# Five places in VectorE's order, in the experts' part of an attention and two-layer mixture-of-experts kernel

## The chip, the cores and the metric

The kernel runs on one core of a Trainium2 chip. The metric is the device time of one execution in microseconds (us), lower is better. TensorE (PE, with its weight loads PEld) multiplies matrices, VectorE (DVE) and ScalarE (ACT) work on elements, GpSimd (POOL) here starts the gathers and scatters by row index, and SyncE (SP) starts the other transfers. Each engine takes its own instructions in the order in which the program lists them and waits for the others by semaphores.

## The reference, cut to what matters

```python
def reference(**kwargs):                       # three layers, one after the other
    attn_out = _attn_ref(**attn_kwargs)        # a gated linear attention, 4 x 8 heads, 768 steps, 48 wide
    x = attn_out.transpose(0, 2, 1, 3).reshape(B * S, H * D)     # 3072 rows of 384
    x = _moe_ref(x=x, **moe_kwargs)            # experts, stage 1
    return _moe2_ref(x=x, **moe2_kwargs)       # experts, stage 2, with a bias on the logits by modality

def _moe_ref(x, w_gate, w1, w2):               # N, D, E, F = 3072, 384, 8, 1024
    logits = x @ w_gate
    expert_idx = np.argmax(logits, axis=1)
    probs = softmax(logits)                    # (a sum of exponentials plus 1e-9)
    gate_w = probs[np.arange(N), expert_idx]
    for e in range(E):
        mask = expert_idx == e
        h = np.maximum(x[mask] @ w1[e], 0.0)
        out[mask] = gate_w[mask, None] * (h @ w2[e])
    return out
```

Each row goes through one expert alone, so the kernel sorts the rows by expert on the chip and works on tiles of 128 rows of one expert.

## The kernel before

**Arithmetic.** The inputs are float32. Each matrix product is made of three float16 products: a number is split into a high half and a low half, and high x high, high x low and low x high are added. So the weights `ws` have a high part `wh` (ScalarE, line 746, 128x768 at a time) and a low part `wl` (VectorE, line 747), and the hidden layer of a tile has `hh` (ScalarE, line 827) and `hl` (VectorE, line 828).

**A tile.** A tile of 128 rows goes through `Stage.steps`: for each quarter q of the 1024 hidden columns, `g1_q` (18 matmuls, into one of three banks `mpq`, `mpk`, `msc`), `hh_q`, `hl_q`, and `g2_q` (six matmuls into `mpu` or `mpy`; the third and the sixth read `hl`). At the end `ev` (VectorE, line 840) makes the factor of each row and `yo` (ScalarE, line 843) scales the output, which POOL scatters. While tile j runs, the kernel also prepares later ones: a gather for tile j+3 (`ga`), the scaling of tile j+2 (`sq` on ScalarE; `sv` on VectorE, lines 775 to 778, four instructions on `ev` and `xs`), the transposes of tile j+1 (`T` on PE; `xh`; `xl`), and the logits of the next layer for the rows that are done (`la` to `ld`).

**Weights.** When the next tile belongs to another expert, the parts of its weights replace the old ones step by step. A part is named by `h` (high) or `l` (low), the matrix (0 for w1, 1 for w2) and the quarter, so `l11` is the low part of the second quarter of w2. Each part stands in an `If` on a register (`Stage.tile`, line 858), since whether the expert changes is known only on the chip. The four last parts (positions of 10 and more in `CHG`) are made in the next tile. SP loads the weights themselves (`refill`).

**Order.** The program order of every engine is written by hand. `POS[stage]` gives each step of a tile a position from about -2 to 10, `CHG[stage]` does so for the weight parts, and `EXT` for everything that stands beside the tiles: an entry's tens count tiles, its rest is the position, and a list holds the positions of the pieces of a generator, one after another. `Stage.tile` sorts all of a tile's pieces by position and emits them, and each engine takes its own in that order.

**Beside the tiles.** `R1` and `R2` are the routers of the two stages. `tabling` makes a table of registers (which expert, whether it changes), in five pieces; `gating` makes the row factors in four: an exponential (ScalarE), eight instructions on VectorE (lines 539 to 547), a strip of 24 or 31 matmuls of 62 columns (PE, line 551), and seven instructions that read it (lines 553 to 562; `ev` and `yo` need what they make).

**Stages and branches.** The first tiles of a stage (two in stage 1, four in stage 2) run "ahead", before the routing is complete, on the expert that is likeliest to come first. `Stage.ahead` then has a branch (line 888) for the case that the guess was wrong; every engine reads a register of the table and passes the branch, and PE's next matmul waits for those engines whose data could have been written in it. `Stage.run` does the remaining tiles. Those from 24 on stand in nested `If`s (line 914), as only the chip knows how many there are; here stage 1 has tiles 0 to 28 and stage 2 tiles 0 to 24. At the end of a stage PE waits again at these `If`s. Stage 1 makes the first weights of stage 2 in its last tile; the parts with positions from 10 on are then made in tile 0 of stage 2, by the entry `wsp`.

Of the kernel before, what the change touches and what calls it, by code (L numbers as in the profile page):

```python
# [25 lines left out]
NT = N // P  # L26
# [78 lines left out]
def attention(tc, ctx, C, q, k, v, a_re, a_im, wg, flags, emit_y, emit_lg, extra, ps, inp):  # L105
# [271 lines left out]


POS=[dict(r1=-1.031,g1_0=0,hh_0=0.547,g1_1=0.882,hl_0=1.39,la=2.05,hh_1=2.196,g1_2=2.293,g2_0=2.443,lc=2.732,hl_1=3.114,r2=4.038,hh_2=4.156,T=4.338,
    g2_1=4.65,xh=4.8,hl_2=4.8,xl=5.173,sq=5.3,g1_3=5.65,hh_3=5.721,lb=5.802,g2_2=6.338,sv=6.511,lt=6.833,ga=6.883,ev=7.217,hl_3=7.445,ld=7.7,  # L380
    g2_3=8.105,yo=9.966),
    dict(la=-2.149,ga=-2.099,r1=-1.063,g1_0=-0.801,g1_1=-0.106,hh_0=1.2,hh_1=2.2,hl_0=2.367,hl_1=2.614,g1_2=2.928,T=3.282,r2=3.634,g2_0=3.64,lc=3.664,
    hh_2=4.688,xh=4.798,hl_2=4.8,xl=5.2,g1_3=5.366,sq=5.443,lb=5.487,g2_1=5.99,hh_3=6.083,hl_3=7.1,ev=7.3,g2_2=7.5,lt=7.586,ld=7.7,sv=7.978,g2_3=8.5,
# [4 lines left out]
    dict(h00=1.25,l00=2.555,h01=3.772,l01=3.889,h10=5,l10=5.85,h02=6.908,h11=7.334,l02=7.573,h03=8.381,l11=8.43,l03=9.238,h12=11.713,h13=12.469,l12=12.6,  # L388
    l13=13.5)]

EXT=dict(ga1=[9.894],tab1=[10.675,11.888,14.575,16.434,19.076],sc2=[14.852,16.409],tu2=[17.791,18.391,19.266],
    sc3=[16.942,20.231],gate1=[13.14,22.34,23.74,26.94],bias=[38.314],guess=[7.193,9.387],ec=[1.828,2.259,3.158],es=[5.811,7.12,9.347],eg0=[-0.314],
    eg1=[2.518],eg2=[2.797],eg3=[0.24],esc0=[7.854,8.86],esc1=[9.262,9.598],esc2=[17.6,18.2],esc3=[17.787,19.2],etu0=[10.7,10.819,11.2],etu1=[16.719,
    16.834,17.692],etu2=[20.882,21.035,21.741],etu3=[26.7,26.797,29.053],wsp=[0.41],lgl=[1.567,2.117,4.049,5.381,7.217],bat=[11.965,12.932,13.065,
    16.165],fin2=[15.779,17.6,18.5,21.1,21.3],ga2=[21.761],tab2=[18.791,23.611,24.661,26.111,28.111],scE=[31.762,31.857],tuE=[34.33,34.944,35.562],
    scF=[34.804,36.2],gate2=[33.763,38.234,40.083,40.999],ckw=[5.75,7.75],ck=[8.464])


HINT=1.5; DRAIN=6.9
# [289 lines left out]
class Rot:  # L689
# [3 lines left out]
    def tile(s, *a, **kw):  # L693
        k=s.i%len(s.t); s.i+=1
        return s.get(k)
# [4 lines left out]
class Bufs:  # L700
# [16 lines left out]
    def rest(s, sb):  # L717
        sh=lambda n,shape,dt,nm: Rot(n,lambda k: sb.tile(shape,dt,name=f"{nm}{k}",tag=f"{nm}{k}",bufs=1))
        s.xg=sh(4,[P,DM],F32,"xg"); s.xs=sh(2,[P,DM],F32,"xs"); s.ev=sh(4,[P,4],F32,"ev")
        s.xh=sh(2,[P,ND,P],F16,"xh"); s.xl=sh(2,[P,ND,P],F16,"xl")  # L720
        s.yo=sh(3,[P,DM],F32,"yo"); s.lxT=sh(6,[P,ND,P],F32,"lxT")
# [27 lines left out]
class Stage:  # L749
# [98 lines left out]
    def tile(s, j, mid=(), old=None, chg=None, refill=False, **kw):  # L848


        W=s.W
        st=[(s.pos[k],f) for k,f in s.steps(j,**kw).items()]

        for k,p in s.chg.items():
            c=old if p>=10 else chg
            if c is None: continue
            def part(c=c,k=k):
                with s.tc.If(c["hl".index(k[0])]!=0): W.split(((int(k[1]),int(k[2])),),**{"lo" if k[0]=="h" else "hi":False})  # L858
            st.append((p%10,part))
        if refill:  # L860
            rf=s.refill(j-1)
            for k in ("r1","r2"): st.append((s.pos[k],lambda: next(rf)))
        st.extend(mid)
        st.sort(key=lambda t:t[0])
        for _,f in st: f()
# [194 lines left out]
def attention__moe__moe2_kernel(tc, q, k, v, a_re, a_im, w_gate, w1, w2, mid, w_gate2, mbias, out):  # L1060
    nc=tc.nc
    with ExitStack() as ctx:
# [8 lines left out]
        W=Weights(tc,cst)  # L1071
# [62 lines left out]
        with ExitStack() as mctx:  # L1134
# [31 lines left out]
            def logits(j, yo):  # L1166

                st=isinstance(j,int)
                px=rt.tile(); y=yo()
                for d in range(ND): nc.tensor.transpose(px[:,d*P:(d+1)*P],y[:,d*P:(d+1)*P],C.ident)  # L1170
                yield
                xT=bf.lxT.tile(); nc.scalar.copy(xT.rearrange("p d t -> p (d t)"),px[:,:DM])
                yield
                own=not st or j>=NL; pl=None
                if own:
                    pl=rt.tile()
                    for d in range(ND): nc.tensor.matmul(pl[:,:E],xT[:,d,:],wg2s[:,d,:],start=(d==0),stop=(d==ND-1))
                else:
                    xTs[j]=xT
                    if j%4==3: grp[0]=group(j-3)  # L1180
                p=(j-3)%4 if st and 3<=j<NL+3 else 3
                if p<3: next(grp[0])
                yield
                if p==0: next(grp[0])
                yield
                if own:
                    js=slice(j,j+1) if st else bass.ds(j,1)
                    nc.vector.tensor_tensor(out=R2.lg[:,js,:].rearrange("p o e -> p (o e)"),in0=pl[:,:E],in1=bias[:,js,:].rearrange("p o e -> p (o e)"),op=ALU.add)
                if p in (1,2): next(grp[0])
                elif st and p==3 and 3<j<NL+3: next(grp[0])  # L1190
                yield
# [6 lines left out]
            H1,H2={},{}  # L1198
            def put(H, nm, f, t=0):

                it=[]
                def step():
                    if not it: it.append(f())
                    next(it[0],0)
                for k in EXT[nm]:
                    j,k=divmod(k+.5,10); H.setdefault(t+int(j),[]).append((k-.5,step))
            def one(f):
                def g():
                    f(); yield
                return g  # L1210
# [9 lines left out]
            for i in range(EK):  # L1220
                put(H1,f"eg{i}",one(lambda i=i: S2.gather(i,exg[i],R2.eids[:,i:i+1])),EN+5)
                put(H1,f"esc{i}",lambda i=i: S2.scaling(i,eev[i],exs[i]),EN+5)
                put(H1,f"etu{i}",lambda i=i: S2.turning(i,exh[i],exl[i]),EN+5)
            put(H2,"wsp",one(lambda: W.split(((1,2),(1,3)))))
            put(H2,"lgl",lambda: logits(S1.last(),lambda: S1.ylast)); put(H2,"bat",lambda: R2.batch(NL,MT-NL,sb,rt,{},imv))
            put(H2,"fin2",lambda: R2.finishing(sb,sb,rt,1.0/(WS*WS),R1.idf))
            put(H2,"ga2",one(lambda: [S2.gather(EK+i) for i in range(3)]))
# [5 lines left out]
            ck=Check(tc,sb,cst,C,fl,W,R1,R2)  # L1233
# [97 lines left out]
```

## Time and profile before

| | |
|---|---|
| median of 3 runs (lowest, highest) | 791.32 us (790.51, 792.84) |
| the profiled execution: its own time | 784.05 us |
| its span, first to last instruction | 782.3 us |
| TensorE busy | 730.2 us, 93% of the span |
| VectorE busy | 533.9 us, 68% |
| ScalarE busy | 474.5 us, 61% |
| mean granted TensorE clock | 0.973 of full speed |
| stage 1 (first and last tile that run after the branch) | 292.66 to 551.97 us |
| stage 2 | from 551.97 us, branch at 591.33 us |

The profiled execution lies 7.27 us under the median of the timed runs. Its row times are from the start of the span. In a row of the timeline the number in square brackets is the time that the engine sat idle before the instruction, with what ended it. A releaser that ends in q (`DVEq`) is an engine's instruction queue: a branch or semaphore instruction there.

### The profile page before, as it was taken

To read this page: it belongs to the slowest core of one execution; us is meant where nothing else is said; L and a number is where in the kernel's file an instruction comes from. 1 tells how busy PE (TensorE), PEld (TensorE's weight loads), DVE (VectorE), ACT (ScalarE), POOL (GpSimd) and SP (SyncE) were. 2 spreads that over 40 slices of the span, in tenths; PEclk is the share of its full clock that TensorE was granted. 3 is DMA by queue.
4 is the path that set the end of the run, shared out by engine and by line. 5 is a ranking of instruction groups with operands and counts; after the bars stand their busy time and mean duration, and the time that the engine had idled before them with its cause. 6 is when DMAs were issued, how large, how long until landed. Compare 5 with 4: busy or idle time off the path is not lost. (4 is left out here: it accounts for less than half of the span.)

```text
span 782.3 us, 23431 instructions
## 1 busy us (share of the span) xinstructions
PE 730.2 (93%) x8451; PEld 587.4 (75%) x8451; DVE 533.9 (68%) x1415; ACT 474.5 (61%) x1007; POOL 297.9 (38%) x289
## 2 busy tenths in 40 slices
PE   7688999899899989999999999999899999999994
PEld 2367878787788867878777878788777878878873
DVE  7888898899789978474747586764564435445354
ACT  7799989798687426374746565675432436434452
POOL 5657788577575231222232224221121222222221
PEclk9799999899899999999999999999999999999997
DMA  9979777675231342433525162524033111611111
GB/s 211 221 146 214 174 153 165 118 173 102 62 82 62 98 158 79 165 112 126 165 91 176 61 197 82 194 68 170 19 112 125 59 47 43 222 43 43 63 42 30
DMA packets 159261, 91.40 MB, mean 117 GB/s; under 512 B 131804, under 2 KB 149764, under 8 KB 159104
## 3 DMA queue, kind: packets, MB, share of 16 engines
q1 hardware_dynamic: 151872, 68.49, 34.1%
q0 software_dynamic: 7232, 21.05, 8.8%
q8 instruction: 71, 1.16, 0.6%
q14 instruction: 86, 0.70, 0.3%
HBM read 192.54 MB, written 20.84 MB: 273 GB/s over the span
## 5 line engine op out<-in xcount | busy, mean ns | idle before, releaser
L823 PEld LDWEIGHTS <-wh 128*128 128x128 f16 x1296 | 127.6, 98 | 10.8 <-ACTq L888 3.0
L824 PEld LDWEIGHTS <-wh 128*128 128x128 f16 x1296 | 127.6, 98 | 8.2 <-issue 1.4
L825 PEld LDWEIGHTS <-wl 128*128 128x128 f16 x1296 | 127.6, 98 | 0.0
L844 POOL DMA_INDIRECT x<-yo,r1ids x27 | 31.7, 1174 | 181.8 <-ACT yo L843 125.0
L747 DVE SCALAR_TENSOR_TENSOR wl<-ws,wh 128x768 f16<-128x768 f32 x88 | 83.6, 962 | 13.1 <-ACTq L858 7.2
L746 ACT ACTIVATE wh<-ws 128x768 f16<-128x768 f32 x88 | 74.1, 844 | 8.9 <-ACTq L858 5.1
L836 PE MATMUL mpu<-wh,hl 128*128 128x384 f16 x216 | 70.5, 327 | 5.0 <-DVE hl L828 4.3
L836 PEld LDWEIGHTS <-hl 128*128 128x128 f16 x432 | 42.2, 98 | 42.3 <-DVE hl L828 11.8
L836 PE MATMUL mpy<-wh,hl 128*128 128x384 f16 x216 | 70.7, 327 | 2.5 <-DVE hl L828 1.6
L844 POOL DMA_INDIRECT out_dram<-yo,r2ids x21 | 21.0, 1002 | 130.9 <-ACT yo L843 123.8
L834 PE MATMUL mpy<-wh,hh 128*128 128x384 f16 x216 | 70.7, 327 | 0.0
L835 PE MATMUL mpy<-wl,hh 128*128 128x384 f16 x216 | 70.6, 327 | 0.0
L834 PE MATMUL mpu<-wh,hh 128*128 128x384 f16 x216 | 70.4, 326 | 0.0
L835 PE MATMUL mpu<-wl,hh 128*128 128x384 f16 x216 | 70.4, 326 | 0.0
L823 PE MATMUL mpk<-xh,wh 128*128 128x128 f16 x384 | 68.4, 220 | 1.3 <-ACTq L888 1.3
L823 PE MATMUL msc<-xh,wh 128*128 128x128 f16 x384 | 67.6, 219 | 1.3 <-DVEq L888 1.3
L825 PE MATMUL mpk<-xh,wl 128*128 128x128 f16 x384 | 68.4, 220 | 0.0
L824 PE MATMUL mpk<-xl,wh 128*128 128x128 f16 x384 | 68.4, 220 | 0.0
L825 PE MATMUL msc<-xh,wl 128*128 128x128 f16 x384 | 67.6, 219 | 0.0
L823 PE MATMUL mpq<-xh,wh 128*128 128x128 f16 x384 | 67.6, 219 | 0.0
L824 PE MATMUL mpq<-xl,wh 128*128 128x128 f16 x384 | 67.6, 219 | 0.0
L825 PE MATMUL mpq<-xh,wl 128*128 128x128 f16 x384 | 67.6, 219 | 0.0
(512 smaller groups left out, 2230.9 us busy)
## 6 DMA issues: line engine op xcount, KB each, us to landing
ws<-in_moe_w_dram SPq DMA_DIRECT2D x100, 1536.0 KB
ar<-in_a_re_dram SPq DMA_DIRECT2D x24, 192.0 KB
ai<-in_a_im_dram SPq DMA_DIRECT2D x24, 192.0 KB
k<-in_k_dram SPq DMA_DIRECT2D x24, 192.0 KB
q<-in_q_dram SPq DMA_DIRECT2D x24, 192.0 KB
v<-in_v_dram SPq DMA_DIRECT2D x24, 192.0 KB
x<-zero SPq DMA_DIRECT2D x8, 576.0 KB
x<-yt SPq DMA_DIRECT2D x24, 192.0 KB
```

The costliest lines, as they stand in the source:

```text
L746: nc.scalar.activation(H_,S_,AF.Copy,scale=WS,accum_out=s.fl[:,s.n:s.n+1]); s.n+=1
L747: if lo: nc.vector.scalar_tensor_tensor(L_,S_,WS,H_,op0=ALU.mult,op1=ALU.subtract)
L823: nc.tensor.matmul(o,W.h1[:,d,fs],x.h[:,d,:],start=(d==0),stop=False)
L824: nc.tensor.matmul(o,W.h1[:,d,fs],x.l[:,d,:],start=False,stop=False)
L825: nc.tensor.matmul(o,W.l1[:,d,fs],x.h[:,d,:],start=False,stop=(d==ND-1))
L834: nc.tensor.matmul(o,hh[:,r,:],W.h2[:,f,:],start=(f==0),stop=False)
L835: nc.tensor.matmul(o,hh[:,r,:],W.l2[:,f,:],start=False,stop=False)
L836: nc.tensor.matmul(o,hl[:,r,:],W.h2[:,f,:],start=False,stop=(f==NF-1))
L844: nc.gpsimd.indirect_dma_start(out=s.dst,out_offset=bass.IndirectOffsetOnAxis(ap=R.ids[:,j:j+1] if ids is None else ids(),axis=0),in_=y,in ...
```

## The change

1. In stage 1 `hl_3`, VectorE's step for the last quarter, moves from position 7.445 to 6.45: from behind `sv` (6.511) and `ev` (7.217) to ahead of both.
2. A new dictionary `LATE` moves `l11` from position 8.606 (8.43 in stage 2) to 11.5, position 1.5 of the next tile, for tiles 23 and later, in both stages. The last of stage 1 has no next tile, so `wsp` now makes that part too, and in another order: at position 0.41 of stage 2's tile 0 both high parts and `l11`, and at 2.7 both remaining low parts.
3. In stage 2 the gating's second piece (VectorE) moves from tile 3, position 8.234, ahead of the branch, to tile 4, position 2.65; the third (the strip on PE) from tile 4, 0.083, to 6.05, and the fourth from 0.999 to 6.6.
4. In stage 1's tile 1 the table's fourth piece (ten small matmuls on PE) moves from 6.434 to 5.6, and the fifth (three copies on VectorE) from 9.076 to 6.42.

```diff
 POS=[dict(...
-    ...,lt=6.833,ga=6.883,ev=7.217,hl_3=7.445,ld=7.7,
+    ...,lt=6.833,ga=6.883,ev=7.217,hl_3=6.45,ld=7.7,
...
+LATE=dict(l11=11.5)
+
-EXT=dict(ga1=[9.894],tab1=[10.675,11.888,14.575,16.434,19.076],...
+EXT=dict(ga1=[9.894],tab1=[10.675,11.888,14.575,15.6,16.42],...
-    ...,wsp=[0.41],...
+    ...,wsp=[0.41,2.7],...
-    ...,gate2=[33.763,38.234,40.083,40.999],...
+    ...,gate2=[33.763,42.65,46.05,46.6],...
...
-        for k,p in s.chg.items():
-            c=old if p>=10 else chg
-            if c is None: continue
-            def part(c=c,k=k):
-                with s.tc.If(c["hl".index(k[0])]!=0): W.split(((int(k[1]),int(k[2])),),**{"lo" if k[0]=="h" else "hi":False})
-            st.append((p%10,part))
+        when=lambda i,k: LATE.get(k,s.chg[k]) if i>=NT-1 else s.chg[k]
+        for k in s.chg:
+            for c,p in ((chg,when(j,k)),(old,when(j-1,k)-10)):
+                if c is None or not 0<=p<10: continue
+                def part(c=c,k=k):
+                    with s.tc.If(c["hl".index(k[0])]!=0): W.split(((int(k[1]),int(k[2])),),**{"lo" if k[0]=="h" else "hi":False})
+                st.append((p,part))
...
-            put(H2,"wsp",one(lambda: W.split(((1,2),(1,3)))))
+            def rest():
+
+                W.split(((1,2),(1,3)),lo=False); W.split(((1,1),),hi=False)
+                yield
+                W.split(((1,2),(1,3)),hi=False)
+                yield
+            put(H2,"wsp",rest)
```

## Rows read from the trace of the kernel before

**Rows 1.** Who PE waited for, from 266 us on: total, times, longest.
```profile
PE mpu L836 <- DVE hl L828: 4.3, 7, 1.6
```

**Rows 2.** PE's timeline, rows with idle time ahead of them: start, duration, instruction.
```profile
305.49 0.34 PE L836 MATMUL mpu<-wh,hl 128*128 128x384 f16 x1 [1.60 <-DVE hl L828]
...
341.54 0.34 PE L836 MATMUL mpu<-wh,hl 128*128 128x384 f16 x1 [0.40 <-DVE hl L828]
...
415.22 0.34 PE L836 MATMUL mpu<-wh,hl 128*128 128x384 f16 x1 [1.16 <-DVE hl L828]
...
470.99 0.34 PE L836 MATMUL mpu<-wh,hl 128*128 128x384 f16 x1 [0.35 <-DVEq L858]
...
551.97 0.22 PE L823 MATMUL mpq<-exh,wh 128*128 128x128 f16 x1 [1.91 <-DVEq L914]
```

**Rows 3.** VectorE's timeline in tile 6, from `sv` to `hl_3`.
```profile
340.09 0.15 DVE L775 TENSOR_SCALAR ev<-fln 128x1 int32<-128x1 int32 x1
...
341.06 0.42 DVE L828 SCALAR_TENSOR_TENSOR hl<-msc,hh 128x256 f16<-128x256 f32 x1
```

**Rows 4.** ScalarE's timeline in tile 6: `hh_3`.
```profile
339.75 0.38 ACT L827 ACTIVATE hh<-msc 128x256 f16<-128x256 f32 x1 [0.16 <-PE msc L825]
```

**Rows 5.** VectorE's timeline: `hl_1` in tiles 3 and 15.
```profile
310.05 0.42 DVE L828 SCALAR_TENSOR_TENSOR hl<-mpq,hh 128x256 f16<-128x256 f32 x1 [0.44 <-ACT hh L827]
...
419.91 0.42 DVE L828 SCALAR_TENSOR_TENSOR hl<-mpq,hh 128x256 f16<-128x256 f32 x1 [0.15 <-DVEq L858]
```

**Rows 6.** PE's timeline: the first matmul that reads that `hl_1`.
```profile
311.13 0.33 PE L836 MATMUL mpy<-wh,hl 128*128 128x384 f16 x1
...
420.86 0.33 PE L836 MATMUL mpy<-wh,hl 128*128 128x384 f16 x1
```

**Rows 7.** Timelines of ScalarE, VectorE and PE in tile 21 and on.
```profile
478.49 0.38 ACT L827 ACTIVATE hh<-msc 128x256 f16<-128x256 f32 x1 [0.77 <-PE msc L825]
...
478.99 0.42 DVE L828 SCALAR_TENSOR_TENSOR hl<-msc,hh 128x256 f16<-128x256 f32 x1
...
482.23 0.55 PE L788 MATMUL mpL<-ident,exs 128*128 128x128 f32 x3
```

**Rows 8.** Timelines at the end of stage 1: VectorE, and PE's weight loads.
```profile
550.04 1.82 DVE L747 SCALAR_TENSOR_TENSOR wl<-ws,wh 128x768 f16<-128x768 f32 x2
...
550.83 0.10 PEld L823 LDWEIGHTS <-wh 128*128 128x128 f16 x1 [1.15 <-ACTq L914]
```

**Rows 9.** Timelines around stage 2's branch: VectorE, PE's weight loads, PE.
```profile
588.39 0.41 DVE L539 TENSOR_REDUCE rfsm<-rfex 128x31 f32<-128x248 f32 x1
...
589.97 1.26 DVE L547 TENSOR_TENSOR r2AQ<-rfA,rfq 128x961 f16<-128x961 f16 x2
...
590.90 0.10 PEld L823 LDWEIGHTS <-wh 128*128 128x128 f16 x1 [1.29 <-ACTq L888]
...
591.33 0.22 PE L823 MATMUL msc<-xh,wh 128*128 128x128 f16 x1 [1.34 <-DVEq L888]
```

**Rows 10.** Timelines in stage 2's tile 4: PE (strip, then `g2_2` and `g2_3`), VectorE.
```profile
593.34 3.48 PE L551 MATMUL mpT<-r2AQ,r2boh 128*128 128x62 f16 x31
...
597.97 0.42 DVE L828 SCALAR_TENSOR_TENSOR hl<-msc,hh 128x256 f16<-128x256 f32 x1
...
602.60 0.33 PE L834 MATMUL mpy<-wh,hh 128*128 128x384 f16 x1
...
603.58 0.33 PE L834 MATMUL mpy<-wh,hh 128*128 128x384 f16 x1
```

**Rows 11.** Stretches: length, busy time of each engine, granted clock, DMA share, GB/s.
```profile
305.00:400.00 95.00, 93.70 (x1167) 76.33 (x1168) 59.25 (x167) 53.94 (x137) 25.36 (x22) 1.00 0.43 141
...
549.00:556.00 7.00, 4.87 (x46) 4.42 (x46) 5.03 (x8) 3.63 (x10) 1.73 (x1) 0.76 0.07 23
```

**Rows 12.** Timelines of tile 5: VectorE's `hl_3` and ScalarE's `yo`.
```profile
331.46 0.42 DVE L828 SCALAR_TENSOR_TENSOR hl<-mpk,hh 128x256 f16<-128x256 f32 x1
...
333.12 0.58 ACT L843 ACTIVATE yo<-mpy,ev 128x384 f32<-128x384 f32 x1 [1.69 <-PE mpy L836]
```

More of the change, by code (lines that the diff above doesn't have):

```diff
@@ L379 @@
 POS=[dict(r1=-1.031,g1_0=0,hh_0=0.547,g1_1=0.882,hl_0=1.39,la=2.05,hh_1=2.196,g1_2=2.293,g2_0=2.443,lc=2.732,hl_1=3.114,r2=4.038,hh_2=4.156,T=4.338,
-    g2_1=4.65,xh=4.8,hl_2=4.8,xl=5.173,sq=5.3,g1_3=5.65,hh_3=5.721,lb=5.802,g2_2=6.338,sv=6.511,lt=6.833,ga=6.883,ev=7.217,hl_3=7.445,ld=7.7,
+    g2_1=4.65,xh=4.8,hl_2=4.8,xl=5.173,sq=5.3,g1_3=5.65,hh_3=5.721,lb=5.802,g2_2=6.338,sv=6.511,lt=6.833,ga=6.883,ev=7.217,hl_3=6.45,ld=7.7,
     g2_3=8.105,yo=9.966),
@@ L389 @@
     l13=13.5)]
-EXT=dict(ga1=[9.894],tab1=[10.675,11.888,14.575,16.434,19.076],sc2=[14.852,16.409],tu2=[17.791,18.391,19.266],
+LATE=dict(l11=11.5)
+EXT=dict(ga1=[9.894],tab1=[10.675,11.888,14.575,15.6,16.42],sc2=[14.852,16.409],tu2=[17.791,18.391,19.266],
     sc3=[16.942,20.231],gate1=[13.14,22.34,23.74,26.94],bias=[38.314],guess=[7.193,9.387],ec=[1.828,2.259,3.158],es=[5.811,7.12,9.347],eg0=[-0.314],
     eg1=[2.518],eg2=[2.797],eg3=[0.24],esc0=[7.854,8.86],esc1=[9.262,9.598],esc2=[17.6,18.2],esc3=[17.787,19.2],etu0=[10.7,10.819,11.2],etu1=[16.719,
-    16.834,17.692],etu2=[20.882,21.035,21.741],etu3=[26.7,26.797,29.053],wsp=[0.41],lgl=[1.567,2.117,4.049,5.381,7.217],bat=[11.965,12.932,13.065,
+    16.834,17.692],etu2=[20.882,21.035,21.741],etu3=[26.7,26.797,29.053],wsp=[0.41,2.7],lgl=[1.567,2.117,4.049,5.381,7.217],bat=[11.965,12.932,13.065,
     16.165],fin2=[15.779,17.6,18.5,21.1,21.3],ga2=[21.761],tab2=[18.791,23.611,24.661,26.111,28.111],scE=[31.762,31.857],tuE=[34.33,34.944,35.562],
-    scF=[34.804,36.2],gate2=[33.763,38.234,40.083,40.999],ckw=[5.75,7.75],ck=[8.464])
+    scF=[34.804,36.2],gate2=[33.763,42.65,46.05,46.6],ckw=[5.75,7.75],ck=[8.464])
 HINT=1.5; DRAIN=6.9
```

## The prediction

> **What bounds the kernel now.** The page comes first: TensorE is busy for 93% of the span and no other engine for more than 68%, so the change can pay only where PE stands still, or loses its clock. The next view is who PE waited for, in the experts' part. It lists little: `hl` seven times [rows 1], two stage branches, the end of stage 1 and a last check that the change doesn't touch. Third is PE's timeline with the idle time ahead of each instruction [rows 2]: the `hl` waits are nearly all at `hl_3`, in the tiles that also make new weights. There VectorE is a queue without gaps, and `hl_3` stands behind `sv` and `ev`. Last, VectorE's and ScalarE's timelines around each wait show what is late next.
>
> **Part 1, `hl_3` ahead of the scaling.** In tile 6 `sv` and `ev` take 341.06 - 340.09 = 0.97 us ahead of `hl_3` [rows 3]. Its input `hh_3` is done at 339.75 + 0.38 = 340.13 [rows 4], so `hl_3` can start at about 340.18, 0.88 earlier. PE's matmul comes 341.54 - 341.06 = 0.48 after the start of the `hl` that it waits for [rows 2, 3]; I use this distance throughout. The wait of 0.40 goes. Tiles 6, 10 and 18 have the same wait: 1.20 us in all.
>
> VectorE does no less work, however, so in the next tile it stands where it stood while PE comes earlier. Its nearest deadline there is `hl_1`. In tile 15 it starts at 419.91 and PE can read it at 420.39, while it reads at 420.86: 0.47 us to spare [rows 5, 6]. Tile 7 shows the same distance, enough for 0.40. So tile 14's wait of 1.16 [rows 2] (of which an `hl_3` that is 0.97 earlier could take 0.97) gives 0.47. In tile 3 the room is 311.13 - 310.05 - 0.48 = 0.60 [rows 5, 6], so tile 2's wait of 1.60 [rows 2] gives 0.60. Tile 20's 0.35 [rows 2] goes whole: no weights are made in tile 21. Sum: 1.20 + 0.47 + 0.60 + 0.35 = 2.62. If the queue gave way as well, the waits alone would bound it: 1.20 + 0.97 + 1.60 + 0.35 = 4.1.
>
> In tiles without new weights VectorE now stands and waits for `hh_3` while `sv` could have run, so what is queued behind (`sv`, `ev`, logits, an expert tile's early scaling) comes later. In tile 21 `hh_3` ends at 478.87 [rows 7]; `hl_3` can start at 478.92 instead of 478.99, and 0.97 us of `sv` and `ev` come behind it, so all that follows is about 0.90 later. Behind it is the early scaling of stage 2's first tile, `exs`, and PE takes its transposes at 482.23 [rows 7], as soon as `exs` is there, after the first matmuls of tile 22 have filled PE up to then. So PE waits 0.90 us anew. Elsewhere I take nothing: the scaled rows are transposed a tile later, and `yo` comes late enough (the last rival). The part's net gain: 2.62 - 0.90 = 1.72 us; between 0.2 (tiles 2 and 14 give nothing, tile 20 half) and 4.1.
>
> **Part 2, `l11` in the next tile.** At the end of stage 1 VectorE is the last: `l11` and `l03`, 1.82 us together, end at 551.86, and PE starts at 551.97 after standing 1.91 us [rows 2, 8]. Without `l11`, 1.82 / 2 = 0.91 us, VectorE leaves at 550.95 and PE starts at 551.06. ScalarE's own end let PE's weight load go at 550.83 [rows 8], so no more than 551.97 - 550.83 = 1.14 could be had, and 0.91 remains. (`hl_3` earns nothing in this tile, since VectorE's total sets its end.) Between 0.5 (ScalarE's end slips by 0.6, as its branch stands behind `yo`) and 1.14. `l11` itself is hidden: in tile 0 of stage 2 it runs while ScalarE makes the two high parts that the old order waited for, and the other two low parts (1.82) have `g2_0`, `g1_3` and `g2_1` of PE ahead of their first reader, `g2_2`. Without that cover, each costs up to 0.91. In stage 1 the only other tile that it concerns is 25, whose `hl_0` in tile 26 comes 0.91 earlier; PE doesn't wait there now, so nothing.
>
> **Part 3, the gates behind the branch.** Today the eight instructions run from 588.39 to 591.23, PE stands 1.34 us and starts at 591.33, while ScalarE's branch had let its weight load go at 590.90 [rows 9]. With VectorE gone 2.84 us earlier, ScalarE decides: PE at about 590.96, 0.37 gained. Behind the branch the chain is eight instructions, strip, seven instructions, then `hl_3`. From the strip's start to the next `hl` takes 597.97 - 593.34 = 4.63, and 0.48 more to PE: 5.11. PE itself has the strip (3.48), `g2_2` (603.58 - 602.60 = 0.98) and two matmuls of 0.16 [rows 10]: 4.78. So a new wait of 0.33 stands at `hl_3` of tile 4. Net 0.04, taken as nothing; from -0.7 (nothing at the branch and twice the wait) to 0.37. No transfer moves with it.
>
> **Part 4, the table earlier.** Nothing. PE's ten small matmuls change places with others of the same tile, and what ends PE's wait at the branch after tile 1 is ScalarE behind its last output, not the table. `hl_3` there comes behind the three short copies, just in time. SP can issue its weight loads a little earlier; in tile 2 ScalarE's splits wait for PE's transposes, so that isn't worth anything. No row prices it closer; I bound it by one `hl` either way, 0.42 [rows 3].
>
> **The clock.** After the idle 1.91 at the end of stage 1 the granted clock is 0.76 in the seven microseconds from 549 [rows 11]. [...] After tile 2's idle 1.60 [rows 2] the clock stayed at 1.00 [rows 11]. Part 2 leaves an idle time of 1.91 - 0.91 = 1.0, below the one that cost nothing. [...]
>
> [...]
>
> **Sum.** 1.72 + 0.91 + 0 + 0 + 1.7 = 4.3 us. Against the profiled execution's own 784.05 that is 779.7. That execution was 7.3 under the median, which the experts' rows don't explain, so I take the sum off the median: 791.32 - 4.3 = **787.0 us**.
>
> **Rivals.**
> 1. *The forecast*, 787.0: chance 0.38.
> 2. *The clock's loss isn't returned*, because the timed runs don't have it or keep it: 791.32 - 2.6 = 788.7. For it: one execution, and two idle times of similar length (1.60 and 1.91) with different ends. 0.27.
> 3. *VectorE's queue takes it back.* The waits at `hl_3` turn into waits at the next tile's `hl_0` and `hl_1`, and what ends stage 1 is ScalarE. For it: the queue has no gap from `hl_2` of a weight-making tile to `hl_1` of the next, and 0.47 is little room. Then part 1 gives about 0.2, part 2 0.9: 790.2, as good as no change. 0.15.
> 4. *The queue gives way*: ScalarE's steps move up with PE, tile 21 is bound by its gather rather than VectorE, and the whole 4.1 comes, with 1.1, 0.4 and 1.7: 791.32 - 7.3 = 784.0. 0.12.
> 5. *Slower: `ev` too late for `yo`.* In quiet tiles `ev` comes about 0.9 later. In tile 5 `hl_3` starts at 331.46 and `yo` at 333.12 [rows 12]; `hl_3` (0.42), then 0.97 let `yo` start at about 332.9: 0.2 to spare. If it is missed, ScalarE has `yo`, then the next `hh_0`, behind it. Stage 1 has some 19 such tiles; from 4.3 / 19 = 0.23 us each the gain is gone, and at 0.4 each the kernel stands at 791.32 + 7.6 - 4.3 = 794.6. Against it: `hh_0` now waits for PE and has a `g1` and more ahead of its reader. 0.08.
>
> **How the numbers follow.** From no change a measurement of this kernel can tell 0.3%, 2.4 us. Faster by more: the first and fourth, and half of the second (2.6 is at the border), 0.38 + 0.12 + 0.14 = 0.64. Within: the other half and the third, 0.28. Slower: 0.08. The range goes from the fourth's 784.0 to 790.6, just beyond the third: it leaves out the fifth and the tails.
>
> **What the profile will show.** Right, if the idle time ahead of the `hl` matmuls is gone in tiles 6, 10, 14, 18 and 20; if tile 2 keeps some of its 1.60 as a wait at tile 3's `hl_1`, tile 14 as one at tile 15's; if PE stands 1.0 instead of 1.91 at the end of stage 1 and the clock there is 1.00; if a wait of 0.9 for `exs` appears at tile 22; if stage 2's branch ends by ScalarE. Wrong, if `yo` waits for VectorE in quiet tiles, if PE waits for the strip's data in stage 2's tile 4, or if the clock falls after the strip in its new place.

## The result, and the profile after

The changed kernel takes 784.42 us (784.11 to 786.54, 6 runs), the kernel before, timed beside it, 791.76 (789.20 to 792.84, 6 runs). The ratio is 0.9911, 95% interval 0.9892 to 0.9931: about 7 us, 0.9%, faster. It lies inside the predicted range, 2.6 us under the predicted 787.0.

The two profiled executions don't show this gain: their spans are 782.3 us before and 782.4 after. The experiments below found the reason (the rows are in experiment 8): the kernel before takes 782.7 and 783.0 us on two chips and 790.1 and 790.7 on two others, and at one place in tile 6 ScalarE stands 0.18 us in a profile from the first kind and 1.16 in one from the second. By its rows the profile of before came from a chip of the quicker kind, while its timed runs (791.76) are like those of the other. So the rows of after are good for what happens at one place, and not for totals.

Who PE waited for in the kernel after, from 300 to 560 us (total, times, longest):

```profile
PE mpL L790 <- DVEq L861: 2.0, 1, 2.0
PE mpq L825 <- DVEq L917: 1.5, 1, 1.5
PE mpy L838 <- DVE hl L830: 1.3, 3, 0.5
PE mpu L838 <- DVE ev L777: 0.9, 4, 0.2
PE mpt L1173 <- ACT yo L845: 0.9, 2, 0.6
```

The waits at `hl_3` that head [rows 1] are gone; what is left of them is 0.9 us in four pieces (the releaser `ev` is the next instruction behind `hl_3`, the nearest event that the trace has). In their place stand waits at the `hl` of the next tile, 0.49 in tile 11 and 0.20 each in tiles 7, 15 and 19 (for these three the view names no releaser and says "issue"), and waits for `yo` (0.9). The rest of the 1.3, two waits of 0.34 and 0.43 in tile 23, isn't new: before they were 0.8 and 0.4. The single rows that answer to [rows 2], from PE's timeline, and those of the new places:

```profile
305.90 0.33 PE L1173 MATMUL mpt<-ident,yo 128*128 128x128 f32 x1 [0.63 <-ACT yo L845]
...
381.34 0.34 PE L838 MATMUL mpy<-wh,hl 128*128 128x384 f16 x1 [0.49 <-DVE hl L830]
...
414.55 0.34 PE L838 MATMUL mpu<-wh,hl 128*128 128x384 f16 x1 [0.18 <-DVE ev L777]
...
485.46 0.33 PE L790 MATMUL mpL<-ident,exs 128*128 128x128 f32 x1 [1.97 <-DVEq L861]
...
555.76 0.22 PE L825 MATMUL mpq<-exh,wh 128*128 128x128 f16 x1 [1.46 <-DVEq L917]
...
593.46 0.23 PE L825 MATMUL msc<-xh,wh 128*128 128x128 f16 x1 [0.91 <-ACTq L891]
...
604.88 0.34 PE L838 MATMUL mpy<-wh,hl 128*128 128x384 f16 x1 [0.32 <-DVE ev L842]
```

Tile 2's 1.60 has become a wait of 0.63 for `yo`, tile 14's 1.16 is 0.18. Stage 1 ends with 1.46 idle instead of 1.91, and the branch of stage 2 with 0.91 by ScalarE instead of 1.34 [rows 9]. Two waits are new: 1.97 for `exs` at tile 22, and 0.32 in stage 2's tile 4. The stretches answer to [rows 11] (length, PE's busy time, granted clock, DMA share, GB/s):

```profile
305.00:400.00 95.00, 93.11 (x1136) 1.00 0.43 141
486.00:490.00 4.00, 4.00 (x42) 0.57 0.31 98
553.00:560.00 7.00, 5.54 (x71) 1.00 0.06 23
```

The granted clock is 1.00 behind the end of stage 1, where it was 0.76. In this execution it falls instead behind the 1.97 us at tile 22, to 0.57 over the four microseconds from 486.

### The profile page after: what moved, and what is told of

It is laid out like the page before. It is cut to its first block, busy times and chain, and to the rows that moved or that the text cites. A ratio compares the mean times of both kernels' runs of the same rounds, so it can differ in the third digit from the quotient of the medians.

```text
span 782.4 us, 23426 instructions
## 1 busy us (share of the span) xinstructions
PE 730.3 (93%) x8451; PEld 584.0 (75%) x8451; DVE 532.9 (68%) x1415; ACT 470.1 (60%) x1007; POOL 293.1 (37%) x289
## 3 DMA queue, kind: packets, MB, share of 16 engines
q8 instruction: 71, 1.16, 0.6%
## 5 line engine op out<-in xcount | busy, mean ns | idle before, releaser
L846 POOL DMA_INDIRECT x<-yo,r1ids x27 | 28.4, 1052 | 191.7 <-ACT hh L829 81.0
L826 PE MATMUL msc<-xl,wh 128*128 128x128 f16 x384 | 68.4, 220 | 0.0
L830 DVE SCALAR_TENSOR_TENSOR hl<-mpq,hh 128x256 f16<-128x256 f32 x73 | 30.9, 423 | 54.7 <-ACTq L861 21.8
```

The costliest lines, as they stand in the source:

```text
L826: nc.tensor.matmul(o,W.h1[:,d,fs],x.l[:,d,:],start=False,stop=False)
L830: def hl(q=q): nc.vector.scalar_tensor_tensor(hs[q][2],hs[q][0][:,:,:P],0.0,hs[q][1],op0=ALU.max,op1=ALU.subtract)
L846: nc.gpsimd.indirect_dma_start(out=s.dst,out_offset=bass.IndirectOffsetOnAxis(ap=R.ids[:,j:j+1] if ids is None else ids(),axis=0),in_=y,in ...
```

## The experiments

Twelve kernels ran, each also timed against the kernel before on its own chip. On two of the chips before takes 782.7 and 783.0 us, on two others 790.1 and 790.7. Each chip was used at one time only, so what is called a chip's here could also belong to the time.

**1. The kernel before, once more.** No edit.

> The kernel before, unchanged, looked at once more, because its one profiled execution (784.05 us) was 7 us under its timed runs. Both theories: a ratio of 1.000. If the sum of waits and the clock at the end of stage 1 explain the gain, this second profile has the same waits of PE in the experts' part (1.16 in tile 14, 1.60 in tile 2, 1.91 at the end of stage 1) and a span of about 788 to 790 with the extra time in clock falls or stalls spread over the whole kernel. If something that one part of the change removes costs the timed runs 7 us, a single stretch of this profile is longer by several us than in the first one, and that stretch is where the part lies.

Measured: 1.001 (0.9992 to 1.0027). On this chip before takes 782.7, and the profile (span 782.3) has the rows of the first one to 0.2 us: 1.91 idle and a clock of 0.77 at the end of stage 1. So no single stretch of this execution hides 7 us; what the 790 of other chips contains is shown by experiment 8.

**2. `hl_3` ahead of the scaling, alone.**

```
-    ... hl_2=4.8, ... ev=7.217, hl_3=7.445, ld=7.7,
+    ... hl_2=4.8, ... ev=7.217, hl_3=6.45,  ld=7.7,
```

> hl_3 ahead of the scaling, alone. By the prediction's sum: 1.7 us faster (0.2 to 4.1), ratio 0.998. By the trace after, where the wait at tile 22 was 1.97 instead of 0.90 and was followed by 3.4 us at the lower clock (1.7 lost): 2.6 - 2.0 - 1.7 = 1.1 us slower, ratio 1.001. By the theory that this part carries what the timed runs gained: 5 us or more faster, ratio at most 0.994.

Measured: 0.9999 (0.9984 to 1.0014), nothing. PE's timeline of this kernel, rows with idle time, says where the gain went:

```profile
307.16 0.33 PE L1170 MATMUL mpt<-ident,yo 128*128 128x128 f32 x1 [0.64 <-ACT yo L843]
...
381.09 0.34 PE L836 MATMUL mpy<-wh,hl 128*128 128x384 f16 x1 [0.31 <-DVE hl L828]
...
482.77 0.33 PE L788 MATMUL mpL<-ident,exs 128*128 128x128 f32 x1 [1.00 <-DVEq L858]
...
551.99 0.22 PE L823 MATMUL mpq<-exh,wh 128*128 128x128 f16 x1 [2.31 <-DVEq L914]
```

`yo` of tile 3 is 1.10 us earlier than in experiment 1 (313.98 against 315.08), and that is the largest lead that lasts. The waits of 0.40 in tiles 6, 10 and 18 are gone and add nothing to it. It is 1.10 in tile 5 (332.16 against 333.26), 1.06 in tile 8 (359.75, 360.81) and 1.06 in tile 12 (395.83, 396.89). Tile 14 lowers it, from 1.07 in tile 13 to 0.60 in tile 15; it is 0.59 in tile 17 and still 0.59 in tile 20. Behind tile 10 most of the wait comes back as the 0.31 at 381.09, at the `hl` of the next tile. Tile 22 loses 1.00 for `exs` and is then 0.38 behind. At the end of stage 1 what has built up again (0.43 at tile 28's `yo`) becomes waiting: 2.31 idle where it was 1.91, and stage 2 begins at 551.99 instead of 552.13. VectorE's last two low parts end 0.14 us earlier than in experiment 1, and no lead of PE gets past them.

**3. The late part alone** (`LATE`, the loop over the parts, and `rest`, as in the diff of the change).

> The low part of one weight block in the next tile, at the end of stage 1, alone. By the prediction: 0.9 us from the wait and 1.7 from the clock that no longer falls there, 2.6 faster, ratio 0.997; if the timed runs have no clock fall there, 0.9 faster, 0.999. By the theory that this part carries the gain (a fall of the clock that lasts longer in the timed runs than in the profiled one): 5 us or more, ratio at most 0.994.

Measured: 777.42 against 782.68, ratio 0.9937 (0.9917 to 0.9956). This part carries most of the gain. The end of stage 1 in its timeline, and the stretch around it:

```profile
551.14 0.22 PE L825 MATMUL mpq<-exh,wh 128*128 128x128 f16 x1 [1.04 <-DVEq L917]
```

```profile
550.00:557.00 7.00, 5.96 (x88) 1.00 0.07 23
```

PE stands 1.04 instead of 1.91 and keeps its clock. From the last `yo` of stage 1 to the first of stage 2 it is 9.98 us instead of 12.48: 2.5 less, as the prediction had it (0.91 + 1.7). A second difference lies at the very end, which the change doesn't touch: who VectorE and PE waited for in the last check, first before, then the late part alone.

```profile
DVE ckb L1296 <- DVEq L914: 4.5, 1, 4.5
...
PE mpT L1299 <- DVE ckout L1265: 6.0, 1, 6.0
```

```profile
DVE ckb L1305 <- DVEq L917: 1.6, 1, 1.6
...
PE mpT L1308 <- DVE ckout L1274: 3.1, 1, 3.1
```

L914 (L917 after) is the chain of branches over the tiles that stage 2 turns out not to need. VectorE jumps over them and then does the check; behind the jump it stands 1.6 us instead of 4.4 to 4.5, and the program ends 2.6 us sooner behind the last `yo` (775.7 - 768.75 = 6.95, against 782.3 - 772.72 = 9.58 in experiment 1). A third difference stands in this profile, 1.5 us around stage 2's strip, where the clock doesn't fall (experiment 4). 2.5 + 2.6 + 1.5 = 6.6, as the two spans differ (782.3 - 775.7); the medians differ by 5.26 (3.4 to 6.5 by the interval), so the timed runs don't show the whole of it.

**4. The gates behind the branch, alone** (`gate2=[33.763,42.65,46.05,46.6]`).

> The gates behind stage 2's branch, alone. By the prediction: 0.37 gained at the branch and 0.33 lost at tile 4, no change, ratio 1.000 (0.4 either way). In the trace before, 3.4 us at the lower clock followed the strip of narrow matmuls in stage 2's tile 4, and the trace after has none there: if that comes from this part, 1.7 faster, 0.998. By the theory that this part carries the gain: at most 0.994.

Measured: 1.0003 (0.9985 to 1.002). In its profile the clock doesn't fall behind the strip, while experiment 1 shows 0.79 from 593 to 601 us:

```profile
593.00:601.00 8.00, 8.00 (x74) 0.79 0.13 40
```

```profile
593.00:601.00 8.00, 8.00 (x85) 1.00 0.10 29
601.00:609.00 8.00, 7.68 (x97) 1.00 0.16 49
```

In this kernel the strip runs from 597 to 601, so the second row is the one behind it. That is 1.56 us in the time from the `yo` of stage 2's tile 3 to that of its tile 4 (13.16 against 14.72). The timed runs show none of it, and in the late part alone, where the strip has its old place, there is no fall either (13.20). In the ten profiles that were read at this place, the fall goes with the one at the end of stage 1 as long as the strip has its old place: the four that have the earlier fall (both of before, the table alone, seven fills fewer) take 14.46 to 14.72 us from the one `yo` to the other, the two that don't (the late part alone, "same places") 13.20 and 13.45. In the strip's new place the four take 13.15 to 13.16, and of these only the gates alone have the earlier fall. So the order of the gates alone doesn't decide this fall, and in the profiles part 2 removes it as well as part 3.

**5. The whole change, and the whole change without part 1**, on one chip with before at 783.0.

> The whole change, beside the kernel before on the chip that timed the parts. If the parts add (0 for hl_3, 5.3 us for the late part, 0 for the gates): 5.3 us faster, ratio 0.993. If hl_3 ahead of the scaling costs more in company than alone (1.97 us at tile 22 instead of 1.00, and the clock's fall behind it, 1.7): about 2.7 less gained, ratio 0.997. By the first measurement of the whole change: 7 us, 0.991.

> The whole change without its first part: hl_3 stays behind the scaling. If the parts add: as the whole change, 5.3 us faster, 0.993. If hl_3 hurts in company: 2.7 us faster than the whole change, and no wait for exs at tile 22 (under 0.3 us), no fall of the clock behind it. By the prediction's sum, in which hl_3 earns 1.7 net: 1.7 us slower than the whole change.

Measured: 776.36, 0.9917 (0.9896 to 0.9937), and 777.17, 0.992 (0.9897 to 0.9942). Between these two the 0.8 us are within the noise; the profiles settle what part 1 does. From the output of stage 1's tile 1 to that of stage 2's tile 0 it is 271.30 us in experiment 1 (291.49 to 562.79) and 271.32 with part 1 alone, 268.79 with the late part alone and 268.79 with the whole change: part 1 gives nothing in company either. The wait for `exs` is 0.99 in the first; in the second its row has none. The first now has a profile of the quicker kind, span 774.7. Against experiment 1 it is 2.19 us shorter at the end of stage 1, 1.56 at the strip, 2.6 behind the last `yo`, 0.3 in stage 1's tiles (with the 2.19 the same 2.5 as in the late part alone), 0.2 longer in stage 2's last tiles; another 1.1 comes from the attention part, where the two pages differ in the granted clock (0.6 against 0.8 in the second of their 40 slices). Sum 7.6, and the spans differ by 782.3 - 774.7 = 7.6.

**6. The jump at the end: is it the place of the code?** Shorter code ahead of the jump, in the order of before; and the late part with as much code added.

```
-    C.zero=...; nc.vector.memset(C.zero,0)      # also chalf, onef
+    C.zero=...; nc.gpsimd.memset(C.zero,0)
```

> The kernel before with three small fills of constants at the program's start made by GpSimd instead of VectorE: VectorE's program is 3 instructions shorter up to the jump over the tiles that are not needed, exactly as much shorter as the late part makes it; the order of the work is that of before. Theory 1, that the late part's gain at the very end (VectorE's idle time of 1.6 us instead of 4.4 to 4.7 behind that jump) comes from where its program's code lies: VectorE's wait behind the jump becomes 1.6, the last check's matmul waits 3.1 instead of 5.8, and the time is 2.8 us lower, ratio 0.9965. Theory 2, that it comes from the order of the work in the last tile: the wait stays at 4.4 or more and the ratio is 1.000.

```
-    C.zero=...; nc.vector.memset(C.zero,0)      # also chalf, onef
+    C.zero=...; nc.vector.memset(C.zero,0); nc.vector.memset(C.zero,0)
```

> The late part alone, with three small fills of constants at the program's start made twice by VectorE (some 0.2 us at a time when VectorE has room): its program is as long as before's up to the jump. Theory 1 (where the code lies): VectorE's idle time behind the jump is 4.4 us or more again, and of the 5.3 us that the late part gained 2.5 are left, ratio 0.997. Theory 2 (the order of the work): it stays at 1.6 and the ratio at 0.9935.

Measured: 1.0011 (0.9996 to 1.0026) with a wait of 4.8, and 0.9951 (0.9934 to 0.9968). The second kernel's last check:

```profile
DVE ckb L1305 <- DVEq L917: 4.7, 1, 4.7
...
PE mpT L1308 <- DVE ckout L1274: 6.2, 1, 6.2
```

Three tiny instructions at the program's start, the order otherwise the same, and the wait at its end goes from 1.6 back to 4.7. What the late part keeps is 3.3 us by the medians (2.5 to 5.2 by the interval); the 2.5 of the end of stage 1 fit, and so would 4.0 with the strip's 1.5. The times alone don't separate the two late kernels (their intervals overlap); the waits do. The first kernel seemed to speak against the place of the code, so two more went after it.

**7. Seven fills fewer, and the same places as in the late part.**

```
-    nc.vector.memset(...)         # zero, chalf, onef, ones, bw, bh, onf
+    nc.gpsimd.memset(...)
```

> The kernel before with seven small fills of constants made by GpSimd instead of VectorE, and nothing else changed. So far VectorE waited 1.6 us behind the jump over the unneeded tiles of stage 2 where that jump is VectorE's 3714th instruction (late part alone, whole change), and 4.4 to 4.8 where it is the 3717th, 3718th or 3721st, whatever the order of the work. Here it is the 3714th. If the place of the jump in VectorE's code decides: 1.6 us behind the jump, the last check's matmul after 3.1 to 3.5 us, and 2.8 us faster than before, ratio 0.9965. If it is the distance to the landing or something else of the late part: 4.4 us or more and 1.000.

```
     s.tile(j,mid,old,chg,refill=j>j0)
+    if s.n==1 and j==MT-1:
+        for _ in range(4): s.tc.nc.vector.memset(s.C.pad,0)
```

> The kernel before, with the seven fills made by GpSimd and four more fills by VectorE in a tile of stage 2 that isn't executed here: VectorE's jump over the unneeded tiles is its 3714th instruction and the landing its 4068th, both as in the late part alone, while everything that is executed goes in the order of before. If the place of VectorE's code alone decides: VectorE waits 1.6 us behind the jump, the last check's matmul 3.1 to 3.5, and the time is 2.8 to 3.3 us lower, ratio 0.996. If the order of the work in the late part is needed too, or the places of the other engines' code: 4.4 us or more, ratio 1.000 to 1.003.

Measured: 1.0028 (1.0004 to 1.0051; some 2 us slower, for which its profile has no place) and 1.0005 (0.9991 to 1.0019), both with a wait of 5.0. The numbers 3714 and 4068 in these expectations come from a listing that leaves out VectorE's register and semaphore instructions. In the full program the late part shortens VectorE's code ahead of the check by 12 instructions, so three or seven fewer fills didn't reach its place. The number of the check's first instruction (the TENSOR_SCALAR_CACHE_REDUCE) in VectorE's full program, beside its wait:

| kernel | number | wait, us |
|---|---|---|
| whole change; late part alone; whole but tile 21 | 7171 | 1.6 |
| late part, three fills more | 7174 | 4.7 |
| before, seven fills fewer | 7175 | 5.0 |
| before, "same places" | 7179 | 5.0 |
| before, three fills fewer | 7180 | 4.8 |
| gates alone | 7182 | 4.7 |
| before; table alone | 7183 | 4.4 to 4.7 |
| part 1 alone | 7184 | 4.7 |

All kernels of the table agree with one border between 7171 and 7174. That the place decides is shown on one side, by the three fills added to the late part. A kernel with before's order and its check at 7171 or less was not run.

The second kernel's profile shows one thing more, at the end of its stage 1:

```profile
559.15 0.22 PE L823 MATMUL mpq<-exh,wh 128*128 128x128 f16 x1 [1.90 <-DVEq L914]
```

```profile
557.00:564.00 7.00, 5.10 (x71) 1.00 0.07 23
```

The same idle time as before, and here the clock stays. Eight profiles have this idle time at 1.9 us or more, and in seven the clock falls behind it; six have 1.0 to 1.5, and it falls in none. At tile 22 the length doesn't sort them: the clock falls behind waits of 1.97 (after) and 2.06 (the table alone), and stays at 1.00 behind 2.13 ("same places"), 2.14 (seven fills fewer) and 2.80 (the whole change with tile 21 in the old order).

**8. The whole change with tile 21 in the old order; the table alone.**

```
-    st=[(s.pos[k],f) for k,f in ...]
+    st=[(7.445 if k=="hl_3" and s.n==0 and j==21 else s.pos[k],f) for k,f in ...]
```

> The whole change, with hl_3 of stage 1's tile 21 alone back behind the scaling, so that exs, which PE's tile 22 transposes, comes 0.9 us earlier. If that wait is what the first part loses: it falls from 1.0 (1.97 in one run) to 0.1 and PE is 0.9 us earlier at tile 23. If VectorE's own work then sets the end of stage 1, the gain comes back as a longer wait there (1.5 becomes 2.0 to 2.4), and with an idle time over 1.9 us the clock falls there again (1.7 us lost): time as that of the whole change or up to 1.7 slower. If PE's lead stays: 0.9 faster than the whole change, ratio 0.9905.

> The table's two last steps in earlier places of their tile, alone. By the prediction: no change, ratio 1.000 (0.4 us either way). A rival: it makes up for what the parts measured so far leave of the whole change (6.5 against 5.3 for the late part alone): 1.2 us faster, 0.9985, with PE's wait at the branch after tile 1 or at tile 2's first hl shorter by that.

Measured: 783.77 against 790.11, 0.9918 (0.9895 to 0.9941); and 1.0014 (0.9992 to 1.0037). The first is no better than the whole change. It ran on a chip of the 790 kind, where the wait for `exs` is 2.80 in spite of the old order (and 2.06 in the table's kernel, whose order there is that of before), so it couldn't test what it was made for: ScalarE is what comes late there. Its timeline in tile 6, first experiment 1, then the table alone, on the other kind of chip:

```profile
335.70 0.19 ACT L746 ACTIVATION_READ_ACCUMULATOR wh<-ws 128x1 f32 x1
336.07 0.38 ACT L827 ACTIVATE hh<-mpq 128x256 f16<-128x256 f32 x1 [0.18 <-ACTq L858]
```

```profile
336.17 0.19 ACT L746 ACTIVATION_READ_ACCUMULATOR wh<-ws 128x1 f32 x1
337.51 0.38 ACT L827 ACTIVATE hh<-mpq 128x256 f16<-128x256 f32 x1 [1.16 <-PE mpk L825]
```

`mpq` was done in both when the accumulator was read. On the second chip ScalarE stands 1.16 us instead of 0.18, behind a branch of the weights' parts. The same comes in tiles 10, 18 and 25 (1.13 to 1.16 instead of 0.18), and 1.2 us more in tile 21 (2.0 instead of 0.77 ahead of `hh_3`). From tile 2's `yo` to tile 28's it is 250.4 us in the kernel with seven fills fewer, which ran on this chip, and 243.8 in experiment 1: 6.6 of the 7.4 us between the two kinds of chip (790.1 - 782.7). Tile 6's `yo` comes 9.39 us after tile 5's on the quicker kind and 10.2 on the other with before's order; in the first profile of before it is 9.38, and in that of after 10.02. So these two profiles are of different kinds, and their spans hide the gain.

## Why the prediction was right, and where not

The time is inside the range, and the sign is right, but the sum of 4.3 us is right in one half only, and something that it didn't have made up for the rest.

**Part 2 and its clock: right.** 0.91 + 1.7 = 2.6 predicted; 2.5 measured in the profile of the part alone, and a gain of 3.3 us (2.5 to 5.2) in the timed kernel whose jump at the end stands where before's did. 0.91 alone lies outside that interval, so the second rival, by which the timed runs don't get the clock back, is unlikely (0.91 and the strip's 1.5, if the timed runs had that, would be 2.4, just outside). No run shows the term 1.7 by itself. In its place the runs show this: the granted clock was 0.50 for 3.4 us behind the 1.91 in the first profile of before (552.4 to 555.8) and 1.00 behind the 1.04 of the late part alone, and of the 2.5 us 0.87 are idle time (1.91 - 1.04) and 1.6 are not. The mean granted clock of the timed runs says the same, though not where a fall lies: its median is 0.979 to 0.983 in the five kernels that have the late part, 0.974 to 0.977 in all others, and with the jump's wait as before (three fills more) 0.979 against 0.975 on the same chip. One fall of 3.4 us to 0.5 is 0.002 of a run. Rival 2's ground was sound in part: one execution of eight kept the clock through the same idle time ("same places": 559.15, 1.90 idle, clock 1.00).

**Part 1: the step that failed.** 1.72 predicted, nothing measured (0.9999). The new wait for `exs` was sized well, 0.90 against 1.00 on the same kind of chip. What failed is the sum of 2.62 from the waits that go: it took each wait as time won for the program. Tile 2 gave more than was counted (1.10 against 0.60, and the rest of its wait is for `yo`, not at tile 3's `hl_1`), but tiles 6, 10, 18 and 20, counted at 1.55, gave nothing that lasts, and tile 14, counted at 0.47, took about as much away. The runs show the third rival in its place, for this part, with one difference: VectorE and not ScalarE ends stage 1. The lead is 1.10 us at tile 3, 0.58 at tile 21 (482.11 against 482.69) and gone at tile 22; what builds up again behind it becomes a longer wait at the end of stage 1 (2.31 against 1.91), since VectorE's own queue ends the stage. The prediction said that of tile 28 alone; it holds for every lead ahead of it. For the same reason the whole change stands 1.46 at the end of stage 1, where 1.0 was predicted and the late part alone has 1.04.

**Parts 3 and 4: right.** The branch ends by ScalarE at 0.91 instead of 1.34 (0.37 expected, 0.43 found), the new wait in tile 4 is 0.32 (0.33 expected); timed, both parts are nothing. The granted clock was 1.00 behind the strip in its new place (593 to 609 us with the gates alone).

**Not in the sum: the jump.** 2.6 us come from VectorE's wait behind the jump over stage 2's unneeded tiles. The prediction took the last check as untouched by the change, and so counted nothing for it; its work is untouched, its place in the program isn't. That the total lies near the forecast is luck to that extent: 1.72 too much stands in the sum, and 2.6 are missing. The fourth rival's 784.0 was met by the number, not by its reason: the queue didn't give way.

**The fifth rival** didn't come: from tile to tile the `yo` of quiet tiles keep their distance (8.70 and 9.48 us before and after).

**Left open:** whether the strip's 1.56 us is part of the timed gain. The late part's profile gains it, but its timed 5.26 is nearer to the sum without it (5.1) than to that with it (6.6); the gates alone don't have it in their times; the whole change's 6.7 has room for it.

## What to carry to other kernels

Waits that end at one queue don't add: before summing what single waits are worth, follow the lead of the engine that waited to the next place where the other engine's total decides, and stop there. Time each part alone before trusting a sum that comes out; here a right total was made of one right part, one that gave nothing and one that nobody had thought of. Where code is added or removed ahead of a long jump, look at the wait behind the jump (1.6 against 4.7 us here).

## What the runs showed of the hardware

- The wait behind the jump over stage 2's unneeded tiles was 1.6 us with the check at instruction 7171 of VectorE's program, and 4.7 with three more instructions ahead of it; over the kernels of the table in experiment 7 it was 1.6 at 7171 and 4.4 to 5.0 at 7174 and more. What VectorE waits for there was not shown.
- The kernel before took 782.7 and 783.0 us on two chips, 790.1 and 790.7 on two others. Of the 7.4 us between the two kinds 6.6 lie in stage 1's tiles (250.4 against 243.8 us from tile 2's `yo` to tile 28's), where ScalarE stood 1.11 to 1.16 us instead of 0.18 in tiles 6, 10, 18 and 25 and 2.0 instead of 0.77 in tile 21. What makes it stand, and whether it belongs to the chip or to the time, is open.
- Behind an idle time of 1.9 us or more at the end of stage 1 the granted clock fell in seven profiles of eight (in the first profile of before to 0.50 for 3.4 us); behind 1.0 to 1.5 in none of six. At another place, tile 22, it fell behind 1.97 and 2.06 and not behind 2.13, 2.14 and 2.80, so the length of the idle time alone doesn't decide it.
- At the strip of narrow matmuls in stage 2, in its old place, the granted clock was 0.79 over 8 us in experiment 1, which has the fall at the end of stage 1, and 1.00 in the late part alone, which hasn't. From the `yo` of tile 3 to that of tile 4 the four profiles read there that have the earlier fall took 14.46 to 14.72 us, the two that haven't 13.20 and 13.45.
